# Loads for a kernel's last column block and transposes for its tap sums, moved in SyncE's queue

## The chip, the cores and the metric

The kernel runs on one core of one Trainium2 chip. Its time is the device time of one execution in microseconds; a kernel is given by the median of its runs. Engines are called TensorE (PE in the profile; PEld is its weight load), VectorE (DVE), ScalarE (ACT), GpSimd (POOL) and SyncE (SP; "SPq" is its queue, in which it issues transfers one after the other).

## What is computed

The reference is a layer made of two branches on one layer-normalised input, and all its gradients. Cut to what matters:

```python
xn = layernorm(x)                       # x: 2048 x 1024, bf16
A  = xn * (conv(kv, ssm_k) + kv * ssm_D)   # kv = shift(k, 4 taps shift_k) * v
B  = (relu(xn @ W_gate) * (xn @ W_up)) @ W_down     # F = 3584
out = x + A + B
# outputs: out, and the gradients by x, k, v, shift_k, ssm_k, ssm_D, W_gate, W_up, W_down
```

The last stage of the kernel makes three of these outputs: the gradient by x, the gradient by shift_k (four "tap sums" for each of 1024 channels, a product of the gradient of the shifted k with k itself, moved by 0 to 3 rows and summed over the 2048 rows) and the gradient by ssm_k (a reordering of values that another stage has stored). It also finishes the last 256 columns of `out` for the last two row tiles.

## The kernel before

All matrices are worked on in tiles of 128 rows. There are 16 row tiles (`ST`), 8 groups of 128 channels (`DT`) and 28 blocks of 128 hidden features (`FT`).

The stages before the last ones compute the hidden layer, the weight gradients and the convolution branch, mixed with each other. After them come two stages:

- `out_phase` (`L1589` on): for each row tile, 28 x 2 matmuls of `hT` (the transposed hidden activations) with `wd` (W_down, held in SBUF whole) into `ps_o`, line L1620. The last two row tiles compute only 768 of the 1024 columns; the other 256 (`REST`) are left for the end of the kernel. Beside this work, SyncE loads W_gate and W_up transposed (`wgT`, `wuT`, L1611).
- `grad_x`: for each row tile `st`, two column halves of 512. For each half 28 matmuls of `ggT` with `wgT` and 28 of `guT` with `wuT`, line L1743, gather in one PSUM tile `ps_x`. VectorE then adds the branch's part and takes the two sums of the layer norm's gradient (L1745, L1747), scales (L1756), ScalarE makes `w` (L1761) and VectorE the result `o` (L1762), which is stored at L1763.

What `grad_x` loads: `ggT` and `guT` are two transposing DMAs for each row tile (`tall`, L1586) into a pool of three buffers that the two share (and that `hT` shares as well). So `guT` of tile 1 goes into the buffer of `ggT` of tile 0, `ggT` of tile 2 into that of `guT` of tile 0, and so on. `gt`, `gy` and `xn` (L1715, L1717, L1719) are plain loads of a row tile each, two buffers each.

From tile 6 (`TAPS_AT`) to tile 13 one channel group per tile is done beside this: three transposing DMAs, `gksT` (L1669), `kT` (L1672) and `ghT` (L1674), are issued for group g+1 after the work of group g has been emitted. `gksT` and `kT` have two buffers, `ghT` one. VectorE multiplies and sums `gksT` with the moved `kT` (L1693, eight instructions for a group), ScalarE reorders `ghT` into `pr` tiles (L1685) that are stored at L1687.

At the end `rest_out` does the last 256 columns of the two last row tiles: 2 x 28 matmuls of `hT` with `wdr` (L1650), an addition (L1654) and a store (L1655). `wdr` is 128 x 28 x 256 (the 256 columns of W_down), loaded by four DMAs at L1632. The `rest` tile holds three pieces of these rows (y, xn, x), three DMAs at L1636, which VectorE multiplies and adds at L1637 and L1638. All of that is emitted by `rest_load`, which `grad_x` calls in tile 1.

What sets the order. The instructions are put in order by a scheduler that goes by a priority (`pri.now()` counts up with every tile) and by when it thinks that an instruction can run. It may thus hoist a DMA past others of the same queue. An instruction that is given to `keep_in_program_order` stays where the program puts it among the instructions of its queue. In the kernel before, `gksT` was held in this way, `kT` and `ghT` were not. On the chip each queue issues strictly in the order that came out: a DMA whose wait is not over holds back all behind it. In the order that was built, `kT` and `ghT` of group 0 and `kT` of group 1 stand directly behind the `rest` loads of tile 1 and ahead of `guT` of tile 1; and in the tap groups a period of SyncE's queue is `guT`, `gksT`, `ghT`, `ggT`, `gy`, `kT` (of the group after), then stores and plain loads.

Of the kernel before, what the change touches and what calls it, by code (L numbers as in the profile page):

```python
# [11 lines left out]
BF16 = mybir.dt.bfloat16  # L12
# [5 lines left out]
P = 128  # L18
# [30 lines left out]
class ABranch:  # L49
# [267 lines left out]
    def load_taps(self, st):  # L317
        skb = st["skb"] = self.sm.tile([P, 4, 1, P], BF16, name="skb")
        self.load(skb[:].rearrange("p i o c -> p (i o c)"),
                  self.sk_d[4 * st["gi"]:4 * st["gi"] + 4, :].rearrange("i c -> (i c)").partition_broadcast(P))  # L320
# [97 lines left out]
    def turn(self, F, b, sign, g=slice(0, 8)):  # L418

        plus, minus = ALU.add, ALU.subtract  # L420
        for i in range(2):
            x = F[:, g, b, i]
            self.tt(x, x, F[:, g, 1 - b, 1 - i], plus if (i == 0) == (sign < 0) else minus)
# [489 lines left out]
class LnMlp:  # L913
# [710 lines left out]
        p_ev.release()  # L1624
        self.p_wd.release()

    def rest_load(self, x, xn_d, y_d, Wd):
        nc, D, c0 = self.nc, self.D, self.D - self.REST
        self.p_rest = self.tc.alloc_tile_pool(name="x_rest", bufs=1, side="right")
        self.wdr = self.p_rest.tile([P, self.FT, self.REST], BF16, name="wdr")  # L1630
        for a in range(0, self.FT, 7):
            nc.sync.dma_start(out=self.wdr[:, a:a + 7, :],  # L1632
                              in_=Wd[a * P:(a + 7) * P, c0:D].rearrange("(kt p) o -> p kt o", p=P))
        t = self.p_rest.tile([P, 3, 2, self.REST], BF16, name="rest")
        for i, src in enumerate((y_d, xn_d, x)):
            nc.sync.dma_start(out=t[:, i], in_=src[(self.ST - 2) * P:self.S, c0:D].rearrange("(t p) o -> p t o", p=P))  # L1636
        nc.vector.tensor_tensor(out=t[:, 0], in0=t[:, 0], in1=t[:, 1], op=ALU.mult)  # L1637
        nc.vector.tensor_tensor(out=t[:, 0], in0=t[:, 0], in1=t[:, 2], op=ALU.add)  # L1638
        self.rest = t

    def rest_out(self, h_d, out0):

# [21 lines left out]
    def load_taps(self, g, gks_d, gh_d, k):  # L1664

        nc, S = self.nc, self.S
        flat = lambda d: d[g].rearrange("p (r c) -> (p r) c", c=P)
        gksT = self.p_tap.tile([P, S], BF16, name="gksT")
        self.tc.keep_in_program_order(nc.sync.dma_start_transpose(out=gksT[:], in_=flat(gks_d)))  # L1669
        kT = self.p_tap.tile([P, 16 + S], BF16, name="kT")  # L1670
        nc.gpsimd.memset(kT[:, 0:16], 0.0)
        nc.sync.dma_start_transpose(out=kT[:, 16:], in_=k[:, g * P:(g + 1) * P])  # L1672
        ghT = self.p_gs.tile([P, S], BF16, name="ghT")
        nc.sync.dma_start_transpose(out=ghT[:], in_=flat(gh_d))  # L1674
        self.rows = gksT, kT, ghT

    def taps(self, g, out_gh, pool):
# [24 lines left out]
    def grad_x(self, x, g, xn_d, y_d, h_d, ug_d, Wd, out0, out1, branch):  # L1702
        nc, tc, D, V = self.nc, self.tc, self.D, self.nc.vector
        p_ev = tc.alloc_tile_pool(name="x_ev", bufs=2, side="right")
        p_sm = tc.alloc_tile_pool(name="x_sm", bufs=2, side="right")
        k, gks_d, gh_d, out_gsk, out_gh = branch
        self.open_taps()
        for st in range(self.ST):
            for _ in range(6):
                self.pri.now()  # L1710
            rows = slice(st * P, (st + 1) * P)
            ggT = self.tall(ug_d[:, 1, :], st, "ggT")
            guT = self.tall(ug_d[:, 0, :], st, "guT")
            gt = p_ev.tile([P, D], BF16, name="gt")
            nc.sync.dma_start(out=gt[:], in_=g[rows, :])  # L1715
            gy = p_ev.tile([P, D], BF16, name="gy")
            nc.sync.dma_start(out=gy[:], in_=y_d[rows, :])  # L1717
            xn = p_ev.tile([P, D], BF16, name="xn")
            nc.sync.dma_start(out=xn[:], in_=xn_d[rows, :])  # L1719
            V.tensor_tensor(out=gy[:], in0=gy[:], in1=gt[:], op=ALU.mult)  # L1720
            if st == 1:
                self.rest_load(x, xn_d, y_d, Wd)
            group = st - self.TAPS_AT
            if 0 <= group < self.DT:
                self.taps(group, out_gh, p_ev)
            if group == self.DT:
                self.store_taps(out_gsk)
            if 0 <= group + 1 < self.DT:
                self.load_taps(group + 1, gks_d, gh_d, k)
            gx = p_ev.tile([P, D], F32, name="gx")  # L1730
            pr = p_ev.tile([P, D], BF16, name="pr")
            w = p_ev.tile([P, D], F32, name="w")
            m = p_sm.tile([P, 10], F32, name="m")
            sums = m[:, 0:6].rearrange("p (a b) -> p a b", b=3)
            hd = tc.keep_in_program_order
            cuts = (0, 512, D)
            for ob in range(len(cuts) - 1):
                oc = slice(cuts[ob], cuts[ob + 1])
                ps = self.ps_tile("ps_x")[:, 0:cuts[ob + 1] - cuts[ob]]
                i, n = 0, 2 * self.FT  # L1740
                for T, W in ((ggT, self.wgT), (guT, self.wuT)):
                    for kt in range(self.FT):
                        nc.tensor.matmul(ps, lhsT=T[:, kt, :], rhs=W[:, kt, oc], start=(i == 0), stop=(i == n - 1))  # L1743
                        i += 1
                V.tensor_tensor_reduce(out=gx[:, oc], in0=ps, in1=gy[:, oc], scale=1.0, scalar=0.0, op0=ALU.add,  # L1745
                                       op1=ALU.add, accum_out=m[:, ob:ob + 1])
                V.tensor_tensor_reduce(out=pr[:, oc], in0=gx[:, oc], in1=xn[:, oc], scale=1.0, scalar=0.0,  # L1747
                                       op0=ALU.mult, op1=ALU.add, accum_out=m[:, 3 + ob:4 + ob])
                if ob:
                    hd(V.tensor_tensor(out=m[:, 6:8], in0=m[:, 6:8] if ob > 1 else sums[:, :, 0], in1=sums[:, :, ob],  # L1750
                                       op=ALU.add))
                if ob + 2 == len(cuts):
                    hd(V.tensor_scalar(out=m[:, 8:10], in0=m[:, 6:8], scalar1=-1.0 / D, scalar2=None, op0=ALU.mult))
                    hd(V.tensor_scalar(out=m[:, 6:8], in0=m[:, 8:10], scalar1=self.rstd[:, st:st + 1], scalar2=None,  # L1754
                                       op0=ALU.mult))
                hd(V.scalar_tensor_tensor(out=gx[:, oc], in0=gx[:, oc], scalar=self.rstd[:, st:st + 1],  # L1756
                                          in1=gt[:, oc], op0=ALU.mult, op1=ALU.add))
            o1 = p_ev.tile([P, D], BF16, name="o1")
            for ob in range(2):
                oc = slice(ob * 512, ob * 512 + 512)  # L1760
                nc.scalar.activation(out=w[:, oc], in_=xn[:, oc], func=ACT.Identity, scale=m[:, 7:8], bias=m[:, 6:7])  # L1761
                V.tensor_tensor(out=o1[:, oc], in0=gx[:, oc], in1=w[:, oc], op=ALU.add)  # L1762
                nc.sync.dma_start(out=out1[rows, oc], in_=o1[:, oc])  # L1763
# [126 lines left out]
```

## Time and profile before

| what | us |
|---|---|
| median of 6 runs | 1869.3 (1865.23 to 1870.67) |
| the profiled execution | 1869.55 |
| its span in the profile | 1867.8 |
| TensorE busy | 1841.0 |
| VectorE busy | 1115.3 |
| ScalarE busy | 630.4 |
| `grad_x`: first and last matmul start | 1466.4 and 1864.4 |
| `grad_x`: one row tile of TensorE's work | 24.17 |

How it is read. A line of a timeline gives the start and the length of a run of instructions in us, the engine, the line of the kernel, the operation, what it writes and reads, how many there are, and in brackets the idle time of the engine just before and what ended it. For a DMA on SyncE's queue the length is that of the issue only; the data lands later. When a DMA landed is taken from the times at which its semaphore was counted up. A line of the table by stretches gives the stretch, the busy time of each engine with the number of instructions, the granted clock of TensorE as a share of the full one, the mean busy share of the DMA engines and GB/s. Ends of matmuls are modelled and overlap, so rows of matmuls are compared by their starts.

### The profile page before, as it was taken

The numbers are of one execution on the slowest core, as the hardware profiler recorded it, in microseconds if no ns is written. First come the engines' busy times: TensorE is split into PE (matmuls) and PEld (weight loads), VectorE is DVE, ScalarE is ACT, GpSimd is POOL, SyncE is SP. The second block draws the span as 40 slices with busy tenths as digits, with TensorE's granted clock in tenths as the row PEclk, the third lists the DMA queues.
The fourth block names the chain that finished last, engine by engine and source line by source line (L and its number), as shares of the span: only waits on it lengthen the run. The fifth ranks groups of instructions, "written<-read, shape, count | busy, mean of one in ns | idle before, by whom it ended". The sixth has DMA issues, their size and how long they took to land.

```text
span 1867.8 us, 31559 instructions
## 1 busy us (share of the span) xinstructions
PE 1841.0 (99%) x12835; PEld 838.7 (45%) x13061; DVE 1115.3 (60%) x1635; ACT 630.4 (34%) x936; POOL 17.0 (1%) x47
## 2 busy tenths in 40 slices
PE   9999999999999999999999999999999999999999
PEld 4444444444444444444444444444444544444444
DVE  6656888798698777684585875711222222466652
ACT  5645444434445445544545354320000000111100
POOL 1000000000000000000000000000000000000000
PEclk9999999999999999999999999999999999999999
DMA  9898499778569748377474363479999955799963
GB/s 258 249 246 175 129 225 231 185 173 205 150 150 239 247 98 208 118 171 241 122 184 132 110 173 121 127 193 271 264 246 237 229 133 131 175 213 197 205 146 74
DMA packets 748370, 344.63 MB, mean 185 GB/s; under 512 B 576072, under 2 KB 715584, under 8 KB 748224
## 3 DMA queue, kind: packets, MB, share of 16 engines
q1 hardware_dynamic: 737568, 321.23, 71.0%
q10 hardware_dynamic: 9216, 16.65, 2.9%
q0 software_dynamic: 1440, 4.72, 0.7%
q8 instruction: 102, 1.67, 0.4%
q14 instruction: 44, 0.36, 0.1%
HBM read 143.79 MB, written 103.83 MB: 133 GB/s over the span
## 4 chain that ended last, share of the span: by engine, by line
PE 95%; SPq 1%; issue 1%; DMA 1%; ACT 1%; DVE 1%; DVEq 0%; ACTq 0%
PE ps_w L1453 20%; PE ps_x L1743 19%; PE ps_h L1120 10%; PE ps_u L1120 10%; PE ps_o L1620 10%; PE ps_g L1120 10%; PE ps_d L1453 9%; PE ps L89 4%; PE ps_d L1468 1%; PE ps_c L89 1%; PE ps_w L1468 0%; DMA guT<-ug_d 0%; SPq L1632 0%; ACT ln_j L987 0%; PE ps_r L1650 0%
## 5 line engine op out<-in xcount | busy, mean ns | idle before, releaser
L1453 PE MATMUL ps_w<-ugs,xn_nat 128*128 128x512 bf16 x1673 | 377.0, 379 | 4.2 <-issue 2.1
L93 ACT CAST arena<-ps 128x1024 bf16<-128x1024 f32 x245 | 239.9, 1020 | 97.4 <-PE ps L89 87.3
L1120 PEld LDWEIGHTS <-xnT 128*128 128x128 bf16 x1792 | 170.7, 98 | 211.7 <-issue 10.6
L339 DVE STREAM_TRANSPOSE arena<-arena 128x1024 f32<-128x1024 f32 x96 | 180.4, 1934 | 132.0 <-ACT arena L93 117.0
L1453 PEld LDWEIGHTS <-xn_nat 128*128 128x128 bf16 x1728 | 164.8, 98 | 203.5 <-issue 11.6
L1120 PE MATMUL ps_u<-wu,xnT 128*128 128x512 bf16 x866 | 204.2, 379 | 2.3 <-issue 1.0
L1120 PE MATMUL ps_g<-wg,xnT 128*128 128x512 bf16 x871 | 203.0, 379 | 3.0 <-DVE xnT L1164 1.0
L1120 PE MATMUL ps_h<-wdT,goT 128*128 128x512 bf16 x868 | 202.0, 379 | 2.0 <-issue 0.8
L1743 PE MATMUL ps_x<-wuT,guT 128*128 128x512 bf16 x878 | 199.2, 381 | 4.5 <-DMA guT<-ug_d 3.5
L1743 PE MATMUL ps_x<-wgT,ggT 128*128 128x512 bf16 x878 | 197.3, 379 | 0.9
L1761 ACT ACTIVATE w<-xn,m 128x512 f32<-128x512 bf16 x32 | 24.3, 807 | 486.2 <-DVE m L1754 372.9
L1620 PE MATMUL ps_o<-wd,hT 128*128 128x512 bf16 (+1 forms) x879 | 186.7, 372 | 0.9
L1453 PE MATMUL ps_d<-g_nat,hs 128*128 128x512 bf16 x742 | 167.8, 379 | 2.4 <-issue 1.6
L1743 PEld LDWEIGHTS <-guT 128*128 128x128 bf16 x896 | 88.0, 98 | 110.7 <-DMA guT<-ug_d 3.9
L1743 PEld LDWEIGHTS <-ggT 128*128 128x128 bf16 x896 | 87.7, 98 | 105.5
L1456 ACT CAST wi<-ps_w 128x512 bf16<-128x512 f32 x108 | 63.6, 589 | 211.0 <-PE ps_w L1453 187.3
L1120 PEld LDWEIGHTS <-goT 128*128 128x128 bf16 x896 | 85.9, 98 | 104.6 <-issue 3.9
L1620 PEld LDWEIGHTS <-hT 128*128 128x128 bf16 x896 | 87.7, 98 | 99.9
L1362 ACT CAST gh<-ps_h 128x512 bf16<-128x512 f32 x112 | 65.5, 585 | 180.9 <-PE ps_h L1120 165.9
L1612 DVE TENSOR_TENSOR ya<-ya,xe 128x1024 bf16<-128x1024 bf16 x16 | 11.1, 692 | 188.5 <-DMA xe<-xn_d 188.5
L1235 DVE SCALAR_TENSOR_TENSOR ru<-ru,ps_u 128x512 bf16<-128x512 bf16 x112 | 76.5, 684 | 78.1 <-PE ps_u L1120 39.3
L97 DVE TENSOR_TENSOR t<-arena 128x2048 bf16<-128x2048 bf16 x96 | 113.8, 1218 | 0.4
(154 smaller groups left out, 1413.4 us busy)
## 6 DMA issues: line engine op xcount, KB each, us to landing
ugs<-ug_d SPq DMA_DIRECT2D x112, 256.0 KB
ug_d<-ru SPq DMA_DIRECT2D x110, 256.0 KB
wg<-in_B_W_gate_dram SPq DMA_DIRECT2D x56, 256.0 KB
wu<-in_B_W_up_dram SPq DMA_DIRECT2D x56, 256.0 KB
h_d<-ht SPq DMA_DIRECT2D x112, 128.0 KB
hs<-h_d SPq DMA_DIRECT2D x56, 256.0 KB
out_dram<-wi SPq DMA_DIRECT2D x56, 256.0 KB
gt<-in_grad_out_dram SPq DMA_DIRECT2D x32, 256.0 KB
```

The source lines that it names most:

```text
L89: self.pri.pin(self.nc.tensor.matmul(out, lhsT=lhsT, rhs=rhs, start=start, stop=stop))
L93: self.pri.pin(self.nc.scalar.copy(out=out, in_=in_))
L97: self.pri.pin(self.nc.vector.tensor_tensor(out=out, in0=in0, in1=in1, op=op))
L339: self.pri.pin(self.nc.vector.transpose(out=df[:, c0:c0 + 32, :], in_=sf[:, c0:c0 + 32, :]))
L1120: self.pri.pin(self.nc.tensor.matmul(ps[:], lhsT=xT[:, kt * P:(kt + 1) * P], rhs=w(kt), start=(kt == 0), stop=(kt == self.DT - 1)), always ...
L1235: return self.pri.pin(nc.vector.scalar_tensor_tensor(out=ru[s][:, 1, :], in0=ru[s][:, 0, :], scalar=0.0, in1=ps[:], op0=ALU.is_gt, op1=ALU ...
L1362: self.pri.pin(nc.scalar.copy(out=gh[:], in_=ps[:]))
L1453: self.pri.pin(self.nc.tensor.matmul(ps[:], lhsT=lhsT(st), rhs=rhs(st), start=(st == 0), stop=(st == self.ST - 1)))
L1456: self.pri.pin(self.nc.scalar.copy(out=out, in_=ps[:]))
L1620: nc.tensor.matmul(ps, lhsT=hT[:, kt, :], rhs=self.wd[:, kt, oc], start=(kt == 0), stop=(kt == self.FT - 1))
L1743: nc.tensor.matmul(ps, lhsT=T[:, kt, :], rhs=W[:, kt, oc], start=(i == 0), stop=(i == n - 1))
L1761: nc.scalar.activation(out=w[:, oc], in_=xn[:, oc], func=ACT.Identity, scale=m[:, 7:8], bias=m[:, 6:7])
```

## The change

Three things move, all in `grad_x`. The transposes for the tap sums, all three of them, are held in SyncE's order. `rest_load` is split: its pools are opened in tile 1, its four pieces of `wdr` are issued in tiles 2, 3, 4 and 5, one in each, and its three loads of rows and the two VectorE instructions come in tile 14. These seven loads are held in SyncE's order as well. No size and no arithmetic is changed, and no buffer is added.

```diff
-    def rest_load(self, x, xn_d, y_d, Wd):
-        nc, D, c0 = self.nc, self.D, self.D - self.REST
+    def rest_open(self):
         self.p_rest = self.tc.alloc_tile_pool(name="x_rest", bufs=1, side="right")
         self.wdr = self.p_rest.tile([P, self.FT, self.REST], BF16, name="wdr")
-        for a in range(0, self.FT, 7):
-            nc.sync.dma_start(out=self.wdr[:, a:a + 7, :],
-                              in_=Wd[a * P:(a + 7) * P, c0:D].rearrange("(kt p) o -> p kt o", p=P))
-        t = self.p_rest.tile([P, 3, 2, self.REST], BF16, name="rest")
+        self.rest = self.p_rest.tile([P, 3, 2, self.REST], BF16, name="rest")
+
+    def rest_weights(self, Wd, i):
+        a, c0 = 7 * i, self.D - self.REST
+        self.tc.keep_in_program_order(self.nc.sync.dma_start(
+            out=self.wdr[:, a:a + 7, :], in_=Wd[a * P:(a + 7) * P, c0:self.D].rearrange("(kt p) o -> p kt o", p=P)))
+
+    def rest_rows(self, x, xn_d, y_d):
+        nc, c0, t = self.nc, self.D - self.REST, self.rest
         for i, src in enumerate((y_d, xn_d, x)):
-            nc.sync.dma_start(out=t[:, i], in_=src[(self.ST - 2) * P:self.S, c0:D].rearrange("(t p) o -> p t o", p=P))
+            self.tc.keep_in_program_order(nc.sync.dma_start(
+                out=t[:, i], in_=src[(self.ST - 2) * P:self.S, c0:self.D].rearrange("(t p) o -> p t o", p=P)))
         nc.vector.tensor_tensor(out=t[:, 0], in0=t[:, 0], in1=t[:, 1], op=ALU.mult)
         nc.vector.tensor_tensor(out=t[:, 0], in0=t[:, 0], in1=t[:, 2], op=ALU.add)
...
-        self.tc.keep_in_program_order(nc.sync.dma_start_transpose(out=gksT[:], in_=flat(gks_d)))
+        turn = lambda out, src: self.tc.keep_in_program_order(nc.sync.dma_start_transpose(out=out, in_=src))
+        turn(gksT[:], flat(gks_d))
         kT = self.p_tap.tile([P, 16 + S], BF16, name="kT")
         nc.gpsimd.memset(kT[:, 0:16], 0.0)
-        nc.sync.dma_start_transpose(out=kT[:, 16:], in_=k[:, g * P:(g + 1) * P])
+        turn(kT[:, 16:], k[:, g * P:(g + 1) * P])
         ghT = self.p_gs.tile([P, S], BF16, name="ghT")
-        nc.sync.dma_start_transpose(out=ghT[:], in_=flat(gh_d))
+        turn(ghT[:], flat(gh_d))
...
             if st == 1:
-                self.rest_load(x, xn_d, y_d, Wd)
+                self.rest_open()
+            if 2 <= st < 6:
+                self.rest_weights(Wd, st - 2)
+            if st == self.ST - 2:
+                self.rest_rows(x, xn_d, y_d)
```

In the order that is built from it, TensorE's, ScalarE's and GpSimd's instructions stand as before. On VectorE the two instructions of `rest` stand with the first half of tile 14 instead of tile 0. On SyncE `guT` of tile 1 comes directly behind `xn` of tile 1; each piece of `wdr` comes directly behind `xn` of its tile, the fourth followed by `gksT`, `kT` and `ghT` of group 0; in the tap groups the period begins `guT`, `gksT`, `kT`, `ghT`, `ggT`, all three of one group; and the three `rest` loads come behind `xn` of tile 14.

## The prediction

> **What bounds the kernel now.** I read the page's first part, then the list of what TensorE waited for over the whole span, then TensorE's timeline around the one entry that matters, and last SyncE's timeline in the same stretch.
>
> ```profile
> PE 1841.0 (99%) x12835; PEld 838.7 (45%) x13061; DVE 1115.3 (60%) x1635; ACT 630.4 (34%) x936; POOL 17.0 (1%) x47
> ```
>
> TensorE is busy for 1841.0 of 1867.8 us. The change takes no matmul away, so it can only win idle time or slowed time of TensorE, and only where its own edits act, in the last stage (`grad_x`, from 1466 us on). The list of waits has one line there, and it is the longest of all lines:
>
> ```profile
> PE ps_x L1743 <- DMA guT<-ug_d: 3.5, 1, 3.5
> ```
>
> ```profile
> 1484.49 6.21 PE L1743 MATMUL ps_x<-wuT,guT 128*128 128x512 bf16 x27
> 1490.53 6.21 PE L1743 MATMUL ps_x<-wgT,ggT 128*128 128x512 bf16 x28
> 1500.19 7.90 PE L1743 MATMUL ps_x<-wuT,guT 128*128 128x512 bf16 x27 [3.46 <-DMA guT<-ug_d]
> 1507.93 6.21 PE L1743 MATMUL ps_x<-wgT,ggT 128*128 128x512 bf16 x28
> ```
>
> Each row is 28 matmuls (a record can be missing). Rows start 6.04 us apart everywhere else in the stage (1484.49 to 1490.53). Here the second half of row tile 1 starts at 1500.19 instead of 1490.53 + 6.04 = 1496.57, which is 3.62 us late, and then takes 7.74 us to the next start instead of 6.04, another 1.70. Together: 17.40 between 1490.53 and 1507.93 where two rows take 12.08, so 5.32 us lost. The second part is the clock, read in stretches of 4 us (the PEclk column):
>
> ```profile
> 1500.00:1504.00 4.00, 3.81 (x10) 1.43 (x11) 0.00 (x0) 0.00 (x0) 0.00 (x0) 0.58 1.16 267
> 1504.00:1508.00 4.00, 3.95 (x19) 1.83 (x19) 0.55 (x1) 0.00 (x0) 0.00 (x0) 1.00 0.70 193
> ```
>
> After the stall the granted clock is half for about 3.4 us, and eight matmuls of this stretch last up to 634 ns against 379. No other row of the stage is off its 6.04 us. Everything that can be won is thus 5.32 us.
>
> Why the stall is there is in SyncE's timeline (start, us, what it issues):
>
> ```profile
> 1474.59 0.43 SPq L1719 DMA_DIRECT2D xn<-xn_d  x1
> 1475.13 6.45 SPq L1632 DMA_DIRECT2D wdr<-in_B_W_down_dram  x4
> 1481.63 1.44 SPq L1636 DMA_DIRECT2D rest<-y_d  x1
> 1483.11 0.47 SPq L1636 DMA_DIRECT2D rest<-xn_d  x1
> 1483.62 0.66 SPq L1636 DMA_DIRECT2D rest<-in_A_q_dram  x1
> 1484.32 3.36 SPq L1672 DMA_TRANSPOSE kT<-in_A_k_dram  x1
> 1487.73 2.45 SPq L1674 DMA_TRANSPOSE ghT<-gh_d  x1
> 1490.22 2.21 SPq L1672 DMA_TRANSPOSE kT<-in_A_k_dram  x1
> 1492.53 4.98 SPq L1586 DMA_TRANSPOSE guT<-ug_d  x1
> ```
>
> `guT` of row tile 1 reuses the buffer of `ggT` of row tile 0, which TensorE releases when its row at 1484.49 begins. The queue reaches it at 1492.53, 8.0 us later, because ten loads stand ahead of it. It lands 7.61 us after that, at 1500.14 (the chain of waits has this piece), and TensorE resumes at 1500.19.
>
> **The change, part by part.**
>
> *Taken from in front of this `guT`.* Four pieces of `wdr` (1475.13 to 1481.58, 6.45 us), three `rest` loads (to 1484.28, 2.65), and `kT`, `ghT`, `kT` (to 1492.43, 8.11): 17.2 us of SyncE. In the built program's order `guT` of tile 1 now comes directly behind `xn` of tile 1, whose issue ended at 1475.02. So it waits for TensorE alone and is issued at about 1484.6. With an idle queue the next `guT` (1514.17) took 5.71 us from issue to its semaphore's last count, so it lands at 1490.3; with the loaded queue's 7.61, at 1492.2. It is needed at 1496.57. The cover is 4.4 to 6.3 us and the stall goes whole: -3.62, and with it the half clock, -1.70.
>
> *What is late next.* `ggT` of tile 2 waits for `guT` of tile 0 (released 1490.53), lands by about 1496.5 and is needed at 1514.7. VectorE no longer stands 6.65 us at the `rest` product; that wait was covered, since its next work from TensorE came at 1490.73. Nothing else waits there.
>
> *Four `wdr` pieces over tiles 2 to 5.* Each stands behind that tile's `xn`. In tiles 2 to 4 SyncE has nothing to do from there to the next `guT`: 1504.03 to 1514.17, 1527.35 to 1538.34, 1550.95 to 1562.52, so 10 to 11.6 us. A piece costs 0.38 (first of the four) to 3.82 us (fourth, behind a full queue); it landed 7.0 to 9.0 us after issue with all four together. Cost on the path: nothing, and 0 even at 3.82. `wdr` is first read after 1858.
>
> *Tile 5 is the tight place.* Here the fourth piece and then all three transposes of the first tap group stand between `xn` (ended 1574.79) and `guT` of tile 6 (due 1586.49): 11.7 us. The piece 0.4 to 3.8, `gksT` 4.33 (its row at 1574.84, behind `gy` and `xn`), `kT` 2.2 to 3.4, `ghT` 1.9 to 3.5: 8.8 to 15.0, I take 10.5, nearest to the rows behind a short queue. `guT` is then late by 0 to 3.3 us. It is needed 12.08 us after it comes due and lands 5.7 to 7.6 after issue, so 1.2 us of cover are left at the worst. Cost: 0.
>
> *The tap groups, tiles 6 to 13.* The old order brought `kT` one group ahead and behind `ggT`; now `kT` comes between `gksT` and `ghT` of its own group. This is where SyncE is nearly full; one period of the kernel before:
>
> ```profile
> 1635.38 4.85 SPq L1586 DMA_TRANSPOSE guT<-ug_d  x1
> 1640.29 2.12 SPq L1669 DMA_TRANSPOSE gksT<-gks_d  x1
> 1642.46 1.87 SPq L1674 DMA_TRANSPOSE ghT<-gh_d  x1
> 1644.42 4.05 SPq L1586 DMA_TRANSPOSE ggT<-ug_d  x1
> ...
> 1649.20 2.24 SPq L1672 DMA_TRANSPOSE kT<-in_A_k_dram  x1
> ...
> 1653.61 5.76 SPq L1687 DMA_DIRECT2D out_dram<-pr  x2
> 1659.46 3.87 SPq L1586 DMA_TRANSPOSE guT<-ug_d  x1
> ```
>
> From `guT` to `guT` it is 24.08 us, against 24.17 of TensorE for a tile. The same instructions stay in the period, so its sum stays. Three things shift by one `kT`, about 2.3 us: `ghT` (landed 1646.89, then 1649.2; ScalarE copies it at 1650.68, and SyncE reads those copies only at 1653.61), `ggT` (needed 24 us after its release) and `gy` (VectorE waits for the later `gt` anyway). `kT`'s buffer was released by VectorE a whole period before, so it brings no new wait; before, its issue at 1649.20 came just behind VectorE's last use. The last tap period (from 1757.49), which had no `kT`, gets one: +2.3 us at most on the `guT` due at 1779.88, which was 0.34 late; with 6.2 to land it has 3.2 us left. Cost: 0; if the cover were gone, each us of a longer period would fall on TensorE.
>
> *The `rest` rows near the end.* They stand behind `xn` of tile 14 (ended 1797.21) with 7.0 us free before `guT` at 1804.25, and cost 2.65. The two products (0.43 us each) follow VectorE's first reduction of tile 14, 25 us later. Cost: 0.
>
> The sum: 1869.55 (the profiled execution; span 1867.8 plus 1.75 around it) - 5.32 = 1864.2. The median of the runs is 0.25 below that execution: 1869.3 - 5.3 = 1864.0.
>
> **A rule weighed against the row.** The Trainium skill, "TensorE: Matmul & The Clock Gate", Part 1 (the HAM clock gate), says that the clock falls to half after at least one idle window of about 3.4 us, that the window runs freely, and that it therefore varies from run to run how much is paid. The idle time here is 3.46 us: by the rule read strictly, a whole window fits into it only by luck, most runs would not pay the 1.70, and the change would win 3.62, giving 1865.7. The row shows that this execution paid it, and it lies 0.25 us from the median, so I count it in: 1864.0. The rule keeps a chance as a rival.
>
> **The rivals.** First, the 1865.7 just worked out: the stall goes, but the median of before did not hold the half clock. For it speaks the low end of the runs, 1865.23; against it that four of the six lie between 1869.05 and 1870.67.
>
> Second, slower. In the tap groups three transposes stand in a row. If a transpose behind another costs what it did behind a full queue (4.33, 3.36, 3.47 = 11.2 against medians of 2.07 + 2.34 + 1.99 = 6.4), the period grows by 4.8 us. Over seven periods that is 33 us, less about 3.8 of cover (a `guT` 1.6 late that takes 6.6 to land, of 12.08): 1864.0 + 29 = 1893. It decides from a growth of 3.8 / 7 = 0.5 us per period, and turns the gain into a loss from (3.8 + 5.3) / 7 = 1.3. Against it: `gksT` and `ghT` already stood in a row and took 1.6 to 3.5.
>
> Third, a small new stall in place of the old one: at tile 5 or the last tap period the cover goes and 2 to 4 us come back: 1866 to 1868.
>
> That the change doesn't do what it says is hardly open: the built order has it, and the matmuls' order is unchanged.
>
> **How the numbers follow.** Full gain 0.70 (1862.8 to 1865.3, the spread of a median); half clock not in the median 0.13; small new stall 0.10; slower by the tap groups 0.07. The likeliest gives 1864.0. The range is 1862.3 to 1867.5: it takes in the first rival and most of the third. About 0.2% (3.7 us, so 1865.6 and 1873.0) is what a measurement of this kernel can tell from no change: faster 0.74, same 0.19, slower 0.07.
>
> **What would show it.** Right: TensorE's row for the second half of tile 1 starts 6.04 us after the one before, no granted clock under 1 in the last stage, no wait for `guT`, `guT` of tile 1 issued about 1484.6, span near 1862.5. Wrong: a TensorE wait for `guT` or `ggT` in tiles 6 to 14, SyncE periods over 24.17 us with `guT` ever later, or single transposes over 3.4 us in the tap groups.

## The result, and the profile after

| | before | changed |
|---|---|---|
| median, us | 1868.35 (39 runs, 1865.23 to 1872.03) | 1864.91 (19 runs, 1863.92 to 1866.0) |
| profiled execution, us | 1869.55 | 1863.95 |
| its span, us | 1867.8 | 1862.2 |
| TensorE busy, us | 1841.0 | 1839.5 |

The ratio is 0.9982 with a 95% interval of 0.9976 to 0.9988: faster by 0.18%, or 3.4 us. The forecast was 1864.0, a gain of 5.3. The two profiled executions differ by 5.6. A twentieth run of the changed kernel, 1866.57 us, is on record and not among the 19; with it the median would be 1864.93.

TensorE's timeline of the changed kernel, the same stretch as before (start, us, what):

```profile
1483.74 6.21 PE L1752 MATMUL ps_x<-wuT,guT 128*128 128x512 bf16 x27
1489.79 6.21 PE L1752 MATMUL ps_x<-wgT,ggT 128*128 128x512 bf16 x28
1495.83 6.21 PE L1752 MATMUL ps_x<-wuT,guT 128*128 128x512 bf16 x27
1501.88 6.21 PE L1752 MATMUL ps_x<-wgT,ggT 128*128 128x512 bf16 x28
```

The row that had started 9.66 us after the one ahead of it (1490.53 to 1500.19) now starts 6.04 after it (1489.79 to 1495.83), and so does the next. No wait for `guT` is left in this stage. The granted clock (PEclk, the column with 1.00) holds:

```profile
1500.00:1504.00 4.00, 4.00 (x20) 1.78 (x19) 2.55 (x6) 0.00 (x0) 0.00 (x0) 1.00 0.35 103
```

SyncE's timeline of the changed kernel, from `xn` of tile 1 to the first piece of `wdr`:

```profile
1473.65 0.43 SPq L1724 DMA_DIRECT2D xn<-xn_d  x1
1483.94 3.60 SPq L1586 DMA_TRANSPOSE guT<-ug_d  x1
...
1496.81 0.42 SPq L1634 DMA_DIRECT2D wdr<-in_B_W_down_dram  x1
```

`guT` of tile 1 is issued 0.2 us after its buffer comes free (the row at 1483.74). By its semaphore it landed at 1489.66, 5.72 after issue, and it was needed at 1495.83. A piece of `wdr` now costs the queue 0.42 us.

The account of the two spans: from the first `ps_x` row to the first `ps_r` row 392.08 before and 386.77 after, that is -5.31, the whole of the stall. The start of `grad_x` came 0.74 earlier (1466.36 and 1465.62), which has nothing to do with the change, and the end from the first `ps_r` row 0.46 later (9.33 and 9.79). Together -5.59.

So the whole stall of the profiled execution is gone, and still the medians differ by 3.4 and not 5.3. That is what the first experiment is about.

### The profile page after: what moved, and what is told of

Its sections match the earlier page's. It is cut to its first block, busy times and chain, and to the rows that moved or that the text cites. A ratio compares the mean times of both kernels' runs of the same rounds, so it can differ in the third digit from the quotient of the medians.

```text
span 1862.2 us, 31568 instructions
## 1 busy us (share of the span) xinstructions
PE 1839.5 (99%) x12835; PEld 838.6 (45%) x13061; DVE 1115.6 (60%) x1635; ACT 630.8 (34%) x936; POOL 17.0 (1%) x47
## 4 chain that ended last, share of the span: by engine, by line
PE 98%; issue 1%; DMA 1%; DVE 0%; ACT 0%; SPq 0%
PE ps_x L1752 21%; PE ps_w L1453 20%; PE ps_h L1120 10%; PE ps_u L1120 10%; PE ps_g L1120 10%; PE ps_o L1620 10%; PE ps_d L1453 9%; PE ps L89 4%; PE ps_d L1468 1%; PE ps_c L89 1%; PE ps_w L1468 0%; PE ps_r L1654 0%; DMA wu<-in_B_W_up_dram 0%; DMA xn_nat<-xn_d 0%; PE pst_x L1159 0%
## 5 line engine op out<-in xcount | busy, mean ns | idle before, releaser
L1120 PEld LDWEIGHTS <-xnT 128*128 128x128 bf16 x1792 | 170.6, 98 | 211.1 <-issue 10.5
```

The lines of the kernel that those rows point to most:

```text
L1120: self.pri.pin(self.nc.tensor.matmul(ps[:], lhsT=xT[:, kt * P:(kt + 1) * P], rhs=w(kt), start=(kt == 0), stop=(kt == self.DT - 1)), always ...
```

## The experiments

Every kernel is compared with runs of the kernel before on the same chip. Two theories stood after the result. S: the loss before is a stall of varying length in every run, with the half clock only in some; the one profile had shown a costly run. F: the loss is the same everywhere, and the changed kernel loses some 2 us where its profile did not catch it.

**The kernel before once more (b_again).** No edit.

> The kernel before, unchanged, to see how its loss varies from run to run. The measured gain was 0.18% (about 3.4 us), less than the 5.3 us of one profiled execution. Theory S (the stall is there in every run, of varying length, and the half clock only in some): the runs lie from about 0.5 to 7 us above those of the changed kernel; runs whose mean granted clock is 1.000 lie some 1.7 us or more lower than those at 0.999; a second profile shows a wait for guT of another length than 3.46. Theory F (the stall is the same 5.3 us in every run, and the changed kernel loses some 2 us elsewhere that its profile did not catch): nearly all runs have a clock of 0.999, and a second profile shows 3.4 to 3.5 us of wait again.

1870.23 us (11 runs) beside 1869.65 (28 runs) of the same kernel, so one and the same within 0.12%. The stretch of its own profile:

```profile
1490.67 6.21 PE L1743 MATMUL ps_x<-wgT,ggT 128*128 128x512 bf16 x28
1499.11 3.66 PE L1743 MATMUL ps_x<-wuT,guT 128*128 128x512 bf16 x11 [2.23 <-DMA guT<-ug_d]
1502.99 4.03 PE L1743 MATMUL ps_x<-wuT,guT 128*128 128x512 bf16 x16 [0.22 <-issue]
1506.85 6.21 PE L1743 MATMUL ps_x<-wgT,ggT 128*128 128x512 bf16 x28
```

The idle time is 2.23 us here and not 3.46, and from 1490.67 to 1506.85 it is 16.18 us against 12.08: 4.10 lost where the first profile had lost 5.32. Over the 28 runs beside it the mean clock splits the times: nine runs at 1.000 lie between 1866.01 and 1868.07 (median 1866.98), nineteen at 0.999 or 0.998 between 1868.15 and 1872.25 (median 1870.18). A half clock of 3.4 us lowers the mean of such a run by 0.0009, so that it is just seen in the third digit. S holds and F falls: a third of these runs of before don't pay the half clock, and the length of the stall moves too. Here `guT` was issued 7.4 us after the release of its buffer (1484.63 to 1492.06) where the first profile had 8.0, and its issue took 4.35 us instead of 4.98. The shorter stall paid the half clock as well: of the 4.10 us, 2.40 are the late start (1499.11 instead of 1496.71) and 1.70 the clock.

**One half of the change at a time (hold_only, loads_only).** The first holds the tap transposes and leaves the loads in tile 1; the second moves the loads and leaves `kT` and `ghT` free.

```diff
 # hold_only, against before
-        nc.sync.dma_start_transpose(out=kT[:, 16:], in_=k[:, g * P:(g + 1) * P])
+        self.tc.keep_in_program_order(nc.sync.dma_start_transpose(out=kT[:, 16:], in_=k[:, g * P:(g + 1) * P]))
...
-        nc.sync.dma_start_transpose(out=ghT[:], in_=flat(gh_d))
+        self.tc.keep_in_program_order(nc.sync.dma_start_transpose(out=ghT[:], in_=flat(gh_d)))
 # loads_only, against the changed kernel: the same two lines the other way round
```

> The transposes for the tap sums held in order, the loads of wdr and rest left in tile 1 ahead of guT. My theory: the three transposes alone (8.1 us of SyncE) made guT late; without them SyncE is through with the rest loads at about 1484.3, when the buffer comes free (1484.5), and guT lands after 7.6 us at the latest, 4 us before it is needed. No wait of TensorE for guT, time within 0.7 us of the changed kernel (1864.9). Rival (the wdr loads' bytes are what delays guT, by filling the DMA queues): a wait of 1 us or more stays, 1866 to 1869.

> The loads of wdr and rest moved as in the change, kT and ghT not held, so that kT, ghT and kT still stand ahead of guT of tile 1. My theory: they are issued from about 1475 to 1483.5, before the buffer comes free at 1484.5, so no wait of TensorE either and a time within 0.7 us of the changed kernel (1864.9): either half of the change is enough. Rival (the transposes ahead are the cause by themselves): a wait of 1 us or more stays, 1866 to 1869. In the tap groups the order is that of before, so SyncE's periods should show whether the new order or something else set them.

1864.79 us (10 runs) and 1864.91 (7 runs), where before had 1869.65: ratios 0.9979 (0.9970 to 0.9988) and 0.9975 (0.9964 to 0.9985). Neither profile has a wait of TensorE in the last stage. SyncE's timeline of hold_only:

```profile
1485.12 0.47 SPq L1636 DMA_DIRECT2D rest<-in_A_q_dram  x1
1487.88 3.55 SPq L1586 DMA_TRANSPOSE guT<-ug_d  x1
```

and of loads_only:

```profile
1484.26 2.01 SPq L1677 DMA_TRANSPOSE kT<-in_A_k_dram  x1
1487.18 3.99 SPq L1586 DMA_TRANSPOSE guT<-ug_d  x1
```

In both, the queue is through before the buffer of `guT` comes free (TensorE's rows at 1487.69 and 1486.98), so it is TensorE and not the queue that `guT` waits for. Either half alone is the whole gain. It is the sum of the ten loads that was too long, and no single one. hold_only takes three transposes out (8.11 us in the profile of before), loads_only the seven plain loads (9.1).

**More and less of the cause (two_ahead, four_ahead).** One transpose fewer ahead of `guT` of tile 1, and one more.

```diff
 # two_ahead, against before: kT of group 0 stays free, kT of the others is held; ghT stays free
-        nc.sync.dma_start_transpose(out=kT[:, 16:], in_=k[:, g * P:(g + 1) * P])
+        ins = nc.sync.dma_start_transpose(out=kT[:, 16:], in_=k[:, g * P:(g + 1) * P])
+        if g:
+            self.tc.keep_in_program_order(ins)
 # four_ahead, against before: in tile 1, all held, guT of this tile issued after them
                 self.rest_load(x, xn_d, y_d, Wd)
+                self.load_taps(0, gks_d, gh_d, k)
+                self.ahead = self.load_k(1, k)
+                guT = self.tall(ug_d[:, 0, :], st, "guT", hold=True)
```

> The kernel before with one transpose fewer ahead of guT of tile 1 (kT of group 1 is held and comes later; kT and ghT of group 0 stay). guT should be issued 2.2 us earlier than before, at about 1490.3, land at about 1497.9 and cost TensorE 1.2 us of idle. Theory S with the clock bound to a long enough stall: no half clock, about 1866.1. Rival (any stall costs the half clock too): 1.2 + 1.7 = 2.9 over the changed kernel, 1867.8.

> The kernel before with one transpose more ahead of guT of tile 1 (gksT, kT, ghT of group 0 and kT of group 1, where before had three). guT should be issued about 2.2 us later than before, at 1494.5, and land at about 1502, so TensorE stands idle 4.5 to 6.5 us. Theory S (the idle time grows with the number of loads ahead, and the half clock of 3.4 us comes once, costing 1.7): idle + 1.7 in the profile, 6.2 to 8.2 over the changed kernel, 1871 to 1873, and nearly all runs at a clock of 0.999 or 0.998. Rival (a longer idle time is punished longer, say two periods of half clock): 1873 to 1875. Rival (no cost of the clock outside the kernel before): 1869.5 to 1871.5.

two_ahead: 1865.89 us (11 runs), all at a mean clock of 1.000, 1.1 over hold_only on the same chip. four_ahead: 1873.13 (10 runs), none at 1.000, 7.6 over the changed kernel's 1865.57 on the same chip. In two_ahead `guT` of tile 1 was issued at 1489.66, 5.0 us after its buffer came free (row at 1484.67), and cost little, since it isn't needed before 12.08 us after that moment. The row of tile 1 in two_ahead:

```profile
1497.37 6.22 PE L1745 MATMUL ps_x<-wuT,guT 128*128 128x512 bf16 x27 [0.45 <-DMA guT<-ug_d]
```

and in four_ahead:

```profile
1505.85 9.06 PE L1754 MATMUL ps_x<-wuT,guT 128*128 128x512 bf16 x28 [8.08 <-DMA guT<-ug_d]
```

Two, three and four transposes ahead give 1.1, 3.2 to 4.9 (before against the changed kernel and its halves, by chip) and 7.6 us of loss. The median of two_ahead came as S had it (1866.1). That of four_ahead, 1873.13, lies just above S's 1871 to 1873, at the low end of the rival by which a longer idle time is punished longer, and the profile sides with that rival: 8.08 idle, and the row takes 2.85 us more than 6.21, where the first profile had shown 1.70. This profile is of a costlier run (1876.85) than the median. Why it lost more is in the last section.

**The changed kernel once more (after_again).** No edit.

> The changed kernel, unchanged, beside the others of this call. Both theories: about 1864.9, every run at a mean clock of 1.000 or nearly so; its spread (about 2 us) comes from the start of the kernel and not from the last stage.

1865.57 us (10 runs, 1864.28 to 1869.08) beside 1868.76: ratio 0.9983 (0.9973 to 0.9992). Nine runs at a clock of 1.000, one, the 1869.08, at 0.999. Where such a run can lose its time is seen in hold_only's profile (1867.81 us, 0.999), which has no wait in the last stage but this at the start of the kernel:

```profile
41.69 5.31 PE L1120 MATMUL ps_g<-wg,xnT 128*128 128x512 bf16 x16 [2.13 <-DVE xnT L1164]
```

In the other profiles these 16 matmuls take 3.63 us after an idle time of 0.6 to 1.1, or come without one. This place belongs to both kernels. It is one source of the rest of the spread; that the run at 1869.08 lost its time there is likely and not shown, as it was not the profiled one.

**How near the tap groups are to their limit (more1, more2).** The slower rival said that the cost would come here, if SyncE's period grew. One or two more transposes stand in each group.

```diff
 # more1 (1) and more2 (2), against the changed kernel; the four wdr pieces all go to tile 14
+        for i in range(1):
+            more = self.wdr[:, 8 * i:8 * i + 8, :].rearrange("p a b -> p (a b)")
+            turn(more, k[:, g * P:(g + 1) * P])
         ghT = self.p_gs.tile([P, S], BF16, name="ghT")
         turn(ghT[:], flat(gh_d))
```

> The changed kernel with one more transpose of kT's size in each tap group, into a buffer that nothing reads before it is overwritten; the four wdr pieces all go to tile 14, so that this buffer is free. It adds about 2.1 us to each of SyncE's periods. The prediction's sum (period 24.08 of 24.17, cover 3.8 us over seven periods): (2.1 - 0.1) x 7 - 3.8 = 10 us slower than the changed kernel, 1875. Theory after the trace of the changed kernel (SyncE has 1 to 2 us to spare in each period, and 5.8 of cover): 0 to 1.5 us slower, 1865 to 1866.5.

> As more1 with two more transposes in each tap group, about 4.2 us for each period. The prediction's sum: (4.2 - 0.1) x 7 - 3.8 = 25 us slower than the changed kernel, 1890. Theory after the trace of the changed kernel: growth of 2.2 to 3.2 us over seven or eight periods, 15 to 26, less 5.8 of cover: 10 to 20 us slower, 1875 to 1885, with waits of TensorE for guT in the last tap groups. Rival (SyncE's queue is hidden whatever is put there): no change, 1865.

1884.35 us (4 runs) and 1900.08 (4 runs): 18.8 and 34.5 over the changed kernel on the same chip, more than either sum had (10 and 25 by the prediction's). A period of SyncE's queue in the changed kernel:

```profile
1653.15 3.69 SPq L1586 DMA_TRANSPOSE guT<-ug_d  x1
...
1662.05 2.32 SPq L1673 DMA_TRANSPOSE ghT<-gh_d  x1
1664.46 3.88 SPq L1586 DMA_TRANSPOSE ggT<-ug_d  x1
...
1671.00 5.04 SPq L1692 DMA_DIRECT2D out_dram<-pr  x2
1677.33 3.58 SPq L1586 DMA_TRANSPOSE guT<-ug_d  x1
```

and in more1:

```profile
1686.36 4.21 SPq L1586 DMA_TRANSPOSE guT<-ug_d  x1
...
1694.93 2.18 SPq L1673 DMA_TRANSPOSE wdr<-in_A_k_dram  x1
1697.17 2.35 SPq L1673 DMA_TRANSPOSE ghT<-gh_d  x1
1699.62 5.03 SPq L1586 DMA_TRANSPOSE ggT<-ug_d  x1
...
1707.36 6.00 SPq L1695 DMA_DIRECT2D out_dram<-pr  x2
1713.78 3.82 SPq L1586 DMA_TRANSPOSE guT<-ug_d  x1
```

In the changed kernel the queue is through at 1676.04, 22.9 us after `guT`, and waits 1.3 us for TensorE. In more1 it is through at 1713.36, 27.0 us after `guT`, and TensorE has long released the buffer (its row at 1705.21). The added transpose takes 2.2 us itself, and the rest of the 4.1 is, net, in other entries: `guT` 0.5 longer, `ggT` 1.1, the two stores of `pr` 1.0 (`gksT` and `kT` 0.8 shorter together). Its seven waits of TensorE for `guT` are 0.55 to 3.22 us, 18.3 in all. The periods from 1605.18 to 1768.15, six of them, average 27.2 against TensorE's 24.17. So the mechanism of the slower rival is real: it starts when the queue's 1.2 us or so to spare and the cover are used up, and one transpose per group is enough for that.

Not all of that round is issuing. The entry of the two `pr` stores holds a wait. In the changed kernel the first store is issued at 1671.00 (0.38 us) and has landed at 1674.46 by its semaphore; ScalarE's copy for the second begins only then, for want of a free `pr` buffer,

```profile
1674.54 1.14 ACT L1690 COPY pr<-ghT 128x512 bf16<-128x512 bf16 x2 [6.24 <-DMA out_dram<-pr]
```

and the second is issued at 1675.70 (0.33 us). SyncE, which issues in order, stands still for 4.2 of the 5.04 us, and in more1 for 5.2 of the 6.00. So of the round of 22.9 us about a fifth is a wait. Whether a third buffer for `pr` would give it back was not tried.

**The order of the tap groups (more1_old, more1_again).** Traces suggested that the new order also shortens SyncE's period: `guT` of the tap groups is issued up to 2.8 us after it comes due in loads_only (old order) and up to 0.6 in hold_only (new order). more1_old is more1 with `kT` and `ghT` free again.

> The same load as more1 (one more transpose in each tap group, into a buffer that nothing reads before it is overwritten; the wdr pieces in tile 14), but kT and ghT not held, so that the tap groups run in the order of the kernel before. Where SyncE's queue was not the limit, its guT came at most 0.6 us late in the new order (hold_only) and up to 2.8 us in the old one (loads_only). If the new order makes SyncE's period shorter by some 0.5 to 1 us, this kernel loses 4 to 7 us more than more1, which was 0.83% over before: 1.0 to 1.3% over before. Rival (the sum of the period is what counts and the order is nothing): 0.8 to 0.9% over before, as more1.

> more1 again, on the same chip as more1_old, for the comparison of the two orders. 0.8 to 0.9% over before (19 us over the changed kernel), with seven or so waits for guT of 0.5 to 3.3 us. The half clock: in the first profile none came after idle times of 2.6 to 3.2 us. If it goes by the length of the idle time alone, none comes here either unless one is longer than 3.4; if by the phase of a running window, some do.

1876.49 us (10 runs, 0.36% over before, 0.23 to 0.50) and 1883.77 (4 runs, 0.69%, 0.54 to 0.84). The expectation has the wrong sign: under the added load the old order loses 7 us less. But the two differ in more than the order. With `kT` free, the added transpose of a group went between `xn` and the stores of `pr` and not between `kT` and `ghT`, two groups' worth of `kT` and of the added one went to tile 1, and the last group's period has neither. One place where they differ is the entry of the two `pr` stores. In more1_old the added transpose stands just ahead of it,

```profile
1650.63 3.72 SPq L1673 DMA_TRANSPOSE wdr<-in_A_k_dram  x1
1654.44 4.07 SPq L1695 DMA_DIRECT2D out_dram<-pr  x2
```

and the entry takes 4.07 to 4.66 us for groups 1 to 6, where more1 has 6.00 to 6.76. By these rows, part of the added transpose goes where the queue would otherwise have waited for ScalarE. From the `guT` at about 1632 on, five rounds average 26.4 us in more1_old, 27.3 in more1 and 27.5 in more1_again. What the order by itself is worth stays open. At the load of the real kernel neither order costs TensorE anything, as hold_only and loads_only show.

## Why the prediction was right, and where its size was off

*The place and the cause.* Right, step by step, and borne out by the runs that take the cause away in halves or add to it: the one wait in the list, the ten loads of SyncE ahead of `guT`, the issue at the release of its buffer (forecast 1484.6, measured 1483.94 with the stage 0.74 earlier), the landing after 5.7 us, nothing late behind it. hold_only and loads_only add that the change is more than was needed: each half leaves the queue free in time. One name is wrong without harm: what the prediction calls the second half of row tile 1 is the `guT` part of its first column half, since a tile has four such rows; the starts and the sums are those of that row.

*The steps costed at nothing.* Right. The four `wdr` pieces took 0.42 us each. In tile 5, the tight place, the piece and the three transposes took 10.7 us (1568.89 to 1579.56) where 10.5 was taken out of 8.8 to 15.0; `guT` of tile 6 was issued at 1580.63, 0.2 us after it came due. In the tap groups the order cost nothing; the last group's `guT` was not late at all, where up to 2.3 us were allowed for.

*The size.* This is the term that was off. The sum took the 5.32 us of one profiled execution as the loss of the median run, because that execution lay 0.25 us from the median of six. Over 39 runs the median of before is 1868.35, one us lower, and a run's loss is not a constant: on the chip of after_again, before at a clock of 1.000 is at 1867.03 (8 runs) and at less at 1870.54 (11 runs), against 1865.57 for the changed kernel, so 1.5 or 5.0 us. What a chip's median shows is a mixture: 3.4 us on the first chip, 3.2 on that of after_again, 4.9 and 4.7 for the two halves; why the chip of the halves has more is not shown. The forecast time, 1864.0, came closer to the measured 1864.91 than the gain did, and that is luck: a start taken 1.0 us too high made up for half of a gain taken 1.9 us too large. The first rival, that the median does not hold the half clock in full, was nearer to the gain on the first chip (3.62) than the forecast, and the weight given to the row over the rule was too large. The rule of the Trainium skill ("TensorE: Matmul & The Clock Gate", Part 1), that what is paid varies from run to run with a window that runs freely, is what the runs show; that an idle time must hold a whole window of 3.4 us is not, since 2.13 us of idle time in a window were enough (last section).

*The slower rival.* It did not come, and its chance was small for the right reason in this kernel (the period's sum was not changed). But its price was too low: by the prediction's sum one more transpose in each group comes to 10 us, and more1 lost 18.8, because a transpose of 2.2 us lengthened the queue's round by 4.1. The prediction also read the 5.76 us of the two `pr` stores as part of what fills the queue; most of such an entry is the wait for ScalarE.

*Faster by over 0.2%* had the highest chance. The measured 0.18% falls short of it, and the interval reaches to both sides of 0.2%.

## What to carry to other kernels

A transfer that waits for a buffer is issued late when the queue ahead of it is not through at the release. Add up the issue times between the last free moment and the release; TensorE stands still only for what of the delay exceeds the cover, the time from the release to the need less that to land (here 8.0 us late, 12.08 to the need, 7.6 to land, 3.6 lost). It is enough to move as many loads as bring the delay under the cover: 8 of 17 us were more than enough. The loss of a stall that the clock can double is not read from one execution: compare several, split by the granted clock, before the gain is put into a number. And a queue that is nearly full in every period is a hard limit though no engine waits for it: one more issue per period cost 19 us here. Look first whether the queue is full of issues or of a wait.

## What the runs showed of the hardware

The clock. All stalls of TensorE of the last stage in the profiles above, by idle time: 3.46, 3.50, 4.70, 5.18, 6.37 and 8.08 us were all followed by a half clock; 2.10 and less never; in between both happened. more1 went through 2.63, 2.79, 2.90, 3.09, 3.14 and 3.22 without one, as this row shows by its 6.22 us,

```profile
1775.25 6.22 PE L1755 MATMUL ps_x<-wuT,guT 128*128 128x512 bf16 x28 [3.22 <-DMA guT<-ug_d]
```

while the same kernel paid 1.7 us after 2.44 in its second profile (more1_again):

```profile
1692.73 7.90 PE L1755 MATMUL ps_x<-wuT,guT 128*128 128x512 bf16 x27 [2.44 <-DMA guT<-ug_d]
1747.61 7.90 PE L1755 MATMUL ps_x<-wuT,guT 128*128 128x512 bf16 x28 [3.50 <-DMA guT<-ug_d]
```

So the length of the idle time alone does not decide. What does decide can be read from the times at which the granted clock changes. more1_again falls to half at 1693.47, 1748.08 and 1802.70, which is 54.61 us apart, or 16 times 3.413; more2 falls at 1670.10, 1728.13, 1758.85 and 1816.88, with 17, 9 and 17 times 3.413 between. A half clock lasts 3.41, 6.83 or 10.24 us, one, two or three such steps. In every one of these profiles the changes lie on a grid of 3.413 us, counted from the first rise of the clock in that execution, which comes anywhere from 4.2 to 7.3 us after the start. Cut along this grid, the stall of 3.22 us in more1 (no half clock), that of 2.44 in more1_again and that of 3.46 in before look like this (after the stretch: TensorE busy; then the granted clock, before the last two columns):

```profile
1770.35:1773.76 3.41, 1.68 (x8) 0.59 (x6) 3.24 (x5) 0.00 (x0) 0.00 (x0) 1.00 1.18 235
1773.76:1777.18 3.42, 1.93 (x9) 0.90 (x10) 3.38 (x9) 0.00 (x0) 0.00 (x0) 1.00 1.04 184
```

```profile
1690.06:1693.47 3.41, 0.96 (x6) 0.39 (x5) 3.24 (x5) 0.00 (x0) 0.00 (x0) 1.00 1.17 250
1693.47:1696.88 3.41, 3.41 (x10) 1.23 (x9) 3.41 (x9) 0.00 (x0) 0.00 (x0) 0.50 1.04 219
```

```profile
1497.20:1500.61 3.41, 0.42 (x2) 0.21 (x3) 0.00 (x0) 0.00 (x0) 0.00 (x0) 1.00 0.99 218
1500.61:1504.03 3.42, 3.42 (x9) 1.22 (x8) 0.00 (x0) 0.00 (x0) 0.00 (x0) 0.50 1.19 276
```

The longer stall was split by the grid into 1.73 and 1.49 us, and the shorter one fell whole into one step. This sorts every wait of TensorE of 0.4 us or more in the twelve profiles from 20 us on, that of hold_only at the start of the kernel too: where the most idle time in one step was 2.13 us or more (eleven cases) the clock was half in the next, and where it was 1.86 or less, never. From this an estimate: a stall of 3.46 us at a random place on the grid pays in about 77 of 100 executions, one of 2.23 in about 40. On the chip of b_again 19 of 28 runs of before were below 1.000.

After 5.18 us and more of idle time a row lost 2.7 to 2.9 us in place of 1.3 to 1.7. In four_ahead the clock was half from 1501.40 to 1511.64, three steps: it fell while TensorE still stood idle, stayed half through the step in which work came back (1.03 us of it idle), and rose only after a step filled with work. After 0.70 us of idle time in such a step (more1_again, 1802.70 to 1806.11) it did rise.

SyncE's queue. In the last stage the issue of one and the same transpose took 3.5 to 5.4 us (`guT`) and 1.7 to 4.6 (`kT`). For `guT` the middle value was 3.7 where the queue had been idle for 1 us or more and 4.2 directly behind another entry. Its semaphore was complete about 2 us after the issue had ended in most cases (`guT` of tile 1 in the changed kernel: issue to 1487.54, landed 1489.66).
